# An expert MLP kernel on one Trainium2 core: the second expert chunk by seven products, the sums of x built in two parts

## The chip, the cores and the metric

The kernel runs on one core of a Trainium2 chip. The metric is device time in microseconds (us) of one execution. The kernel before took 957.64 us, the median of three runs (957.54 to 958.07).

## The reference

Three layers follow one another, on 1536 tokens of 512 numbers. The first is attention in which a query sees the keys of its own cluster; the second is a mixture of 4 experts, weighted by normalised probabilities; the third is a plain two-layer network with a leaky ReLU.

```python
def _moe_ref(x, domain_probs, w1, w2):
    N, D = x.shape                  # 1536, 512
    E = w1.shape[0]                 # 4 experts, F = 1024 hidden units each
    p = domain_probs / (domain_probs.sum(-1, keepdims=True) + 1e-09)
    out = np.zeros((N, D), dtype=np.float32)
    for e in range(E):
        h = np.maximum(x @ w1[e], 0.0)
        out += p[:, e:e + 1] * (h @ w2[e])
    return out.astype(np.float32)

def _moe2_ref(x, w_in, w_out):      # 2048 hidden units
    h = x @ w_in
    g = np.maximum(0.01 * h, h)
    return (g @ w_out).astype(np.float32)

def reference(**kwargs):
...
    x = np.ascontiguousarray(attn_out.transpose(0, 2, 1, 3)).reshape(B * S, H * D)
    x = _moe_ref(x=x, **moe_kwargs)
    return _moe2_ref(x=x, **moe2_kwargs)
```

## The kernel before, in words

Numbers are float32; every large product is done as three matmuls on halves of 16 bits (high x high, high x low, low x high). After the heads of the attention, which take the first 255 us or so, the hidden units of both networks are worked off in 24 chunks of 256: chunks 0 to 15 are the experts' (N1 = 16), 16 to 23 the last network's. Each chunk has a hidden part and an outputs part.

**Hidden part.** A chunk in PLAIN goes through `plain` (L1070): for each of three blocks of 512 tokens (`tokens` cuts them) and two halves of 128 hidden units 12 matmuls of 512 columns, so 72. Chunk 0 is such a chunk; its first two blocks are worked off among the last heads, and its third one behind them. The other chunks go through `emit_seven`: hidden units, input rows and tokens (two halves of HT = 768) are each cut in two, and seven products of half-size matrices take the place of eight. `product` (L1059) issues 6 matmuls for one product. The first factors of four products are sums of weights s1 to s4, the second ones of the four are sums of x, t1 to t4, and the remaining products take quarters of the weights and of x as they are. Slices A (512 tokens of each half) and B (256 of each half) are two matmul groups of one product. Where a chunk isn't `full`, only A goes by products, and `plain_b` does the other 512 tokens by 12 matmuls for each half of the hidden units.

**Hidden values.** `h_act` (VectorE, L790) applies the ReLU and the probabilities pb; ScalarE (L139) makes the high half hhi, POOL (L140) the low half hlo.

**Outputs part.** `emit_y1` (L1195 to L1197) makes 12 tiles of 6 matmuls; ScalarE (L1203, chunk 0) or VectorE (L1205, the others) takes each into acc.

**Weights.** SP loads w1 and w2 of a chunk (L190) into w1raw and w2raw. `peak` (ScalarE, L220, into junk) finds the largest value in each partition, a matmul (L224) spreads it, VectorE (L228 to L212) makes a power of two of it, ScalarE scales by it (L272) and makes the high half (L264), POOL the low half (L267). For `emit_seven` POOL builds the four sums of weights (`weights_sums`, L284 to L287), and `split_halves` makes their halves shi (ScalarE, L264) and slo (POOL, L267). The raw buffer of w1 is free for the next load after L287.

**Sums of x.** `input_sums` (L1003) builds f, g and e, by VectorE (L1013) in float32, and their high halves by ScalarE (L1016), low halves by VectorE (L1013). f and g lie in raw64, two tiles of the pool `ffn` that take up memory of the heads' pool after it is closed (L954); the high and low half of e overwrite the quarter b12 of x, xx in the trace.

**Order of work.** The steps of weights and sums are lists of small functions. The loop over the chunks pops some after each block or output tile, by numbers in `quota`; each engine then runs its instructions in the order in which they were issued. Chunk 0 spreads the 18 steps of the sums by `quota = [0, 9, 6, 3]`: none in chunk 0's hidden part, nine among its outputs, six in chunk 1's hidden part and three among its outputs.

In the trace `junk`, `g`, `hhi` and so on are tiles, `z` a bank of PSUM, `big` a wider part of it.

Of the kernel before, what the change touches and what calls it, by code (L numbers as in the profile page):

```python
# [8 lines left out]
F32 = mybir.dt.float32  # L9
# [4 lines left out]
AF = mybir.ActivationFunctionType  # L14
# [61 lines left out]
def attention_moe_kernel(  # L76
# [13 lines left out]
    nc = tc.nc  # L90
# [92 lines left out]
    def weights_load(c, part):  # L183
        wa, wb, f0, e = chunks[c]
        r, n = (raw64, 2) if wide and e is None else (raw12, 1)
        if part == 0:
            src = wa[:, n * f0:n * (f0 + FCH)]
        else:
            src = wb[f0:f0 + FCH, :]
        nc.sync.dma_start(out=r[part], in_=src.rearrange("(k p) f -> p k f", p=128))  # L190
# [597 lines left out]
    def h_act(c, g, src, p):  # L788
        if c < N1:
            nc.vector.scalar_tensor_tensor(out=g, in0=src, scalar=0.0, in1=p, op0=ALU.max, op1=ALU.mult)  # L790
        else:
            nc.scalar.activation(out=g, in_=src, func=AF.Prelu, scale=H_DOWN, alpha=0.01)
# [9 lines left out]
    def like(x, y):  # L802
        return x if len(y.shape) == 2 else x.rearrange("p (u t) -> p u t", u=2)
# [196 lines left out]

    t_hi, t_lo = [[t[:, 0], t[:, 1], quarters[1][n], t[:, 2]] for n, t in enumerate((thi, tlo))]

    def input_sums():  # L1003

        sub, add = ALU.subtract, ALU.add
        b11, b12, b21, b22 = quarters
        f, g = [
            x.bitcast(F32).rearrange("p a b -> p (a b)")[:, 0:NT].rearrange("p (k t) -> p k t", k=2) for x in raw64
        ]
        e = part  # L1010

        def tt(out, in0, in1, op):
            return lambda: nc.vector.tensor_tensor(out=out, in0=in0, in1=in1, op=op)  # L1013

        def hi(n, src):
            return lambda: nc.scalar.activation(out=t_hi[n], in_=src, func=AF.Copy)  # L1016

        def lo(n, src):
            return tt(t_lo[n], src, t_hi[n], sub)

        return [
            tt(f, b12[0], b11[0], sub), tt(f, f, b12[1], add), tt(f, f, b11[1], sub),
            hi(0, f), tt(g, b22[0], f, sub), tt(g, g, b22[1], add), lo(0, f), hi(1, g), tt(e, b22[0], b12[0], sub),
            tt(e, e, b22[1], add),
            lo(1, g), tt(e, e, b12[1], sub), tt(f, b21[0], g, sub), tt(f, f, b21[1], add), hi(3, f),
            hi(2, e), lo(3, f), lo(2, e),
        ]

    def turn_sums(m):
# [44 lines left out]
    def emit_seven(c, steps, late):  # L1074
# [12 lines left out]
        u2, u3 = [{A: part[:, n, A], B: part[:, n, B]} for n in range(2)]  # L1087
        gB = [g_slot(2), g_slot(3)]

        full = c < N1 or c >= FULL  # L1090
        calls = [5 if full else 6]

        def some():
# [19 lines left out]
        def plain_b(f):  # L1113

            ps = bank(f)
            xs = [x.rearrange("p k (u t) -> p k u t", u=2) for x in (xhi, xlo)]
            for k in range(KC):
                for i, j in ((0, 0), (0, 1), (1, 0)):
                    nc.tensor.matmul(
                        ps.rearrange("p (u t) -> p u t", u=2), lhsT=w[i][:, k, 128 * f:128 * f + 128],  # L1120
                        rhs=xs[j][:, k, :, 512:HT], start=k + i + j == 0, stop=k == KC - 1 and i == 1,
                    )
            h_act(c, gB[f], ps, None)
            hi, lo = [x[:, f, :].rearrange("p (u t) -> p u t", u=2)[:, :, 512:HT] for x in hbuf[0]]
            split(hi, lo, gB[f].rearrange("p (u t) -> p u t", u=2), nc.gpsimd)

# [151 lines left out]
    def mixed(*lists):  # L1278
        return [x for row in zip_longest(*lists) for x in row if x]

    PLAIN = (0, 1, N1, N1 + 1)
    FULL = N1 + 4
    sums_left, quota = [], []
    for c in range(NCH):
# [14 lines left out]
        if c in PLAIN:  # L1299
            if c != N1:  # L1300
                if c > 0:
                    weights_split(c, 1)
                out_scale(c)
            if c == N1:
                sums_left = turn_sums(slice(0, 512))
                quota = [0, 6, 4, 3]
            if c == 0:
                sums_left = input_sums()
                quota = [0, 9, 6, 3]
            n = quota.pop(0)  # L1310
            slots = mixed(sums_left[:n], steps)
            slots[len(slots) // 2:len(slots) // 2] = late[:1]
            if c != N1:
                slots += late[1:]
            sums_left = sums_left[n:]
            if c == N1:
                turn_max(1)
                for k in range(KC):
                    turn_split(1, k)
                weights_split(c, 1)  # L1320
            blocks = [(u, f) for u in range(2 if c == 0 else 0, NU) for f in range(NF)]
            for n, (u, f) in enumerate(blocks):
                if c > 0 and c != N1:
                    ps = bank(BANKS[u][f])
                    plain(c, u, f, ps)
                elif f == 0:
                    both_ps = [bank((BANKS[u] if c else LAST_BANKS)[f]) for f in range(NF)]
                    for k in range(KC):
                        for g in range(NF):
                            plain(c, u, g, both_ps[g], [k])  # L1330
                if c == N1 and n == 0:
                    turn_across(1, bank(1))
                    turn_scale(1)
                    for k in range(KC):
                        turn_split(2, k)
                    out_scale(c)
                if c == 0 or c == N1:
                    ps = both_ps[f]
                h_whole(c, f, ps, 512 * u, hl=[tokens(x[:, f], c, u, True) for x in hbuf[0]])
                if c == N1 and n < 2:  # L1340
                    continue
                for _ in range(-(-len(slots) // (len(blocks) - n))):
                    slots.pop(0)()
            left = []
        else:
            emit_seven(c, steps, late)
            left = steps

        steps, later = left, []
        if c == N1 + 2:  # L1350
            sums_left = turn_sums(slice(512, HT))
            quota = [5, 8]
        if c in PLAIN or N1 + 2 <= c < FULL:
            n = quota.pop(0)
            later, sums_left = sums_left[:n], sums_left[n:]
        if more:
            if not is_wide(c + 1):
                later.insert(0, lambda: peak(c + 1, 1))
            else:
                if c + 1 != N1:  # L1360
                    later.insert(0, lambda: peak(c + 1, 1))
                if c == N1:
                    later = late[1:] + later
                if c + 2 < NCH:
                    later.append(lambda: weights_load(c + 2, 1))
            if L1_POINT(c):
                steps.append(lambda: weights_split(c + 1, 0))
            else:
                steps.insert(0, None)
            if c + 1 not in PLAIN:  # L1370
                steps += weights_sums()
            if c + 2 < NCH and not is_wide(c + 2):
                steps.append(lambda: weights_load(c + 2, 0))
        if c == N1 - 3 and wide:
            steps += [lambda: weights_load(N1, 0), lambda: weights_load(N1, 1)]
        if c < N1 - 1 and c % (FE // FCH) == FE // FCH - 1:
# [66 lines left out]
```

## Time and profile before

| | |
|---|---|
| median of three runs | 957.64 us |
| profiled execution, device time | 957.7 us |
| its span, first to last instruction | 955.8 us |
| TensorE busy | 98% of the span |
| share of the chain that ended last | TensorE 84%, VectorE 11% |
| granted TensorE clock | full speed in every slice |
| chunk 0's third block | 250.02 to 255.20 us |
| chunk 0's outputs | 255.20 to 270.85 us |
| chunk 1's hidden part, its outputs | 270.85 to 286.39, 286.39 to 302.04 us |

The span is taken by the hardware profiler; the device time of the same execution has 1.9 us around it. Busy times are sums of an engine's instructions; the rows further down show when each engine worked, and "idle before" with an arrow names what ended the idle time. A duration is that of one instruction or, with x2 or more behind it, of several in a row, and neighbouring instructions of one engine can overlap by up to 0.1 us.

### The profile page before, as it was taken

What the parts mean: (1) busy time and instruction counts of PE and PEld (TensorE: products, weight loads), DVE (VectorE), ACT (ScalarE), POOL (GpSimd) and SP (SyncE); (2) the same over time, 40 slices, a digit from 0 to 9 for tenths busy, and PEclk for the clock granted to TensorE, in tenths of its full rate; (3) what the DMA queues carried; (4) which work ended last, traced back from release to release, by engine and by line L of the source; (5) the groups of instructions that cost most, each with busy time, mean ns of one, the idle gap of its engine ahead of it and who ended that gap; (6) DMA issues with size and microseconds to landing.
All of it is one profiled execution on the core that took longest, in us unless ns stands there. A gap on an engine that the chain in (4) does not pass through costs nothing.

```text
span 955.8 us, 16375 instructions
## 1 busy us (share of the span) xinstructions
PE 938.0 (98%) x6423; PEld 552.2 (58%) x6456; DVE 749.0 (78%) x1286; ACT 536.8 (56%) x775; POOL 564.1 (59%) x456
## 2 busy tenths in 40 slices
PE   8899999999999999999999999999999999999998
PEld 5788888877545555555555555555544444455554
DVE  7989998889697676666766667666889978998865
ACT  3678777778555344334344343443579755566552
POOL 4467777780367565455654465654636667777672
PEclk9999999999999999999999999999999999999999
DMA  8785556550110112110211102114111211221103
GB/s 181 182 186 120 129 131 156 122 135 3 45 45 25 42 47 54 45 45 23 61 40 45 45 23 75 37 33 132 45 45 59 94 54 60 88 89 45 45 1 132
DMA packets 62245, 70.81 MB, mean 74 GB/s; under 512 B 28148, under 2 KB 44920, under 8 KB 62168
## 3 DMA queue, kind: packets, MB, share of 16 engines
q1 hardware_dynamic: 62168, 69.77, 27.0%
q8 instruction: 50, 0.82, 0.4%
q14 instruction: 27, 0.22, 0.1%
HBM read 46.19 MB, written 3.17 MB: 52 GB/s over the span
## 4 chain that ended last, share of the span: by engine, by line
PE 84%; DVE 11%; ACT 2%; DMA 1%; issue 1%; SPq 0%; DVEq 0%; ACTq 0%
PE z L1059 27%; PE z L1195 9%; PE z L1196 8%; PE z L1197 8%; PE z L1257 4%; PE z L1259 4%; PE z L1258 4%; PE z L1070 4%; PE big L508 3%; DVE m L512 2%; PE big L543 2%; PE big L544 2%; PE small L569 1%; PE small L570 1%; PE small L571 1%
## 5 line engine op out<-in xcount | busy, mean ns | idle before, releaser
L140 POOL TENSOR_TENSOR hlo<-g,hhi 128x512 bf16<-128x512 f32 x140 | 186.4, 1354 | 89.9 <-ACT hhi L139 89.9
L1205 DVE SCALAR_TENSOR_TENSOR acc<-z,outer,acc 128x512 f32<-128x512 f32 x180 | 133.8, 748 | 64.7 <-PE z L1197 64.7
L557 POOL TENSOR_TENSOR plo<-p,phi 128x768 f16<-128x768 f32 x83 | 136.2, 1652 | 68.3 <-ACT phi L556 38.6
L139 ACT ACTIVATE hhi<-g 128x512 f16<-128x512 f32 x140 | 86.6, 628 | 111.8 <-DVE g L790 110.2
L1195 PE MATMUL z<-hhi,w2hi 128*128 128x512 f16 x384 | 145.5, 379 | 1.6
L1196 PE MATMUL z<-hhi,w2lo 128*128 128x512 f16 x384 | 145.5, 379 | 0.0
L267 POOL TENSOR_TENSOR w2lo<-w2raw,w2hi 128x512 f16<-128x512 f32 x46 | 63.5, 1400 | 131.5 <-ACT w2hi L264 131.5
L1197 PE MATMUL z<-hlo,w2hi 128*128 128x512 bf16 x353 | 133.8, 379 | 0.0
L512 DVE TENSOR_REDUCE m<-big 128x1 f32<-128x768 f32 x96 | 89.9, 950 | 14.0 <-PE big L508 13.7
L546 ACT ACTIVATE p<-big 128x768 f32<-128x768 f32 x96 | 76.6, 808 | 34.6 <-PE big L544 28.6
L1059 PEld LDWEIGHTS <-shi 128*128 128x128 f16 x608 | 59.5, 98 | 41.3 <-issue 0.2
L1099 DVE TENSOR_TENSOR part<-z,part 128x512 f32<-128x512 f32 x76 | 41.2, 563 | 50.9 <-PE z L1059 48.3
L267 POOL TENSOR_TENSOR w1lo<-w1raw,w1hi 128x512 f16<-128x512 f32 x46 | 57.4, 1270 | 28.5 <-ACT w1hi L264 18.8
L1059 PE MATMUL z<-xx,shi 128*128 128x512 f16 (+1 forms) x304 | 73.1, 329 | 0.1
L1257 PE MATMUL z<-w2hi,hhi 128*128 128x512 f16 (+1 forms) x194 | 73.1, 377 | 0.1
L1059 PE MATMUL z<-xx,w1hi 128*128 128x512 f16 (+1 forms) x304 | 73.1, 329 | 0.0
L1259 PE MATMUL z<-w2hi,hlo 128*128 128x512 f16 (+1 forms) x194 | 73.1, 377 | 0.0
L1258 PE MATMUL z<-w2lo,hhi 128*128 128x512 f16 (+1 forms) x194 | 73.1, 377 | 0.0
L543 PE MATMUL big<-qka 128*128 128x512 f32 x192 | 70.0, 367 | 2.8 <-DVE m L512 1.2
L1266 DVE SCALAR_TENSOR_TENSOR accn<-z,outer,accn 128x512 f32<-128x512 f32 (+1 forms) x85 | 60.2, 736 | 14.5 <-PE z L1259 14.4
L264 ACT ACTIVATE shi<-sums 128x1024 f16<-128x1024 f32 x20 | 21.1, 1057 | 88.4 <-POOL sums L287 88.4
L790 DVE SCALAR_TENSOR_TENSOR g<-z,pb 128x512 f32<-128x512 f32 x92 | 51.7, 568 | 19.2 <-PE z L1059 11.4
(250 smaller groups left out, 2342.7 us busy)
## 6 DMA issues: line engine op xcount, KB each, us to landing
qkb<-pair SPq DMA_DIRECT2D x32, 384.0 KB
w1raw<-in_moe_w_dram SPq DMA_DIRECT2D x16, 512.0 KB
w2raw<-in_moe_w_dram SPq DMA_DIRECT2D x16, 512.0 KB
w1raw<-in_moe_w_in_dram SPq DMA_DIRECT2D x8, 1024.0 KB
w2raw<-in_moe_w_out_dram SPq DMA_DIRECT2D x8, 1024.0 KB
qka<-pair SPq DMA_DIRECT2D x16, 384.0 KB
qraw<-in_q_dram SPq DMA_DIRECT2D x16, 192.0 KB
kraw<-in_k_dram SPq DMA_DIRECT2D x16, 192.0 KB
```

The source lines that it names most:

```text
L140: lo_engine.tensor_tensor(out=lo, in0=src, in1=as_read(hi), op=ALU.subtract)
L267: nc.gpsimd.tensor_tensor(out=lo[:, x], in0=src[:, x], in1=hi[:, x], op=ALU.subtract)
L512: nc.vector.tensor_reduce(out=m_t[t][:, j:j + 1], in_=ps[:, 0:S], op=ALU.max, axis=AX.X)
L557: (nc.vector if plo_on_vector else nc.gpsimd).tensor_tensor(out=plo, in0=p, in1=phi, op=ALU.subtract)
L1059: nc.tensor.matmul(ps, lhsT=w[i][:, k, :], rhs=x[j][:, k, sub], start=first and k + i + j == 0, stop=k == 1 and i == 1, skip_group_check=True,
L1195: nc.tensor.matmul(out, lhsT=whi[:, f, ks], rhs=h, start=f == 0, stop=False)
L1196: nc.tensor.matmul(out, lhsT=wlo[:, f, ks], rhs=h, start=False, stop=False)
L1197: nc.tensor.matmul(out, lhsT=whi[:, f, ks], rhs=l, start=False, stop=f == NF - 1)
L1205: nc.vector.scalar_tensor_tensor(out=a, in0=out, scalar=by, in1=a, op0=ALU.mult, op1=ALU.add)
L1257: nc.tensor.matmul(ps, lhsT=hi[:, f, ts], rhs=whi[:, f, m], start=f == 0, stop=False)
L1258: nc.tensor.matmul(ps, lhsT=hi[:, f, ts], rhs=wlo[:, f, m], start=False, stop=False)
L1259: nc.tensor.matmul(ps, lhsT=lo[:, f, ts], rhs=whi[:, f, m], start=False, stop=f == NF - 1)
```

## The change

Chunk 1 leaves PLAIN and goes through `emit_seven`, but not `full`: slice A by seven products, the other 512 tokens by `plain_b`, whose `h_act` is now given the probabilities in expert chunks. The sums of x are built by `input_sums(m)` for a slice m of the tokens. Slice A is built in chunk 0: its first five steps ahead of the third block, the other 13 among the outputs (quota 16). Slice B is built in chunk 1: eight steps in the hidden part, ten among the outputs. e lies in acc_n instead of part. The sums of weights of chunk 1 are built among chunk 0's outputs, so the load of chunk 2's w1 goes out after them.

```diff
@@ -1000,30 +1000,29 @@
 
     t_hi, t_lo = [[t[:, 0], t[:, 1], quarters[1][n], t[:, 2]] for n, t in enumerate((thi, tlo))]
 
-    def input_sums():
+    def input_sums(m):
 
         sub, add = ALU.subtract, ALU.add
-        b11, b12, b21, b22 = quarters
-        f, g = [
-            x.bitcast(F32).rearrange("p a b -> p (a b)")[:, 0:NT].rearrange("p (k t) -> p k t", k=2) for x in raw64
+        b11, b12, b21, b22 = [[x[:, :, m] for x in b] for b in quarters]
+        f, g, e = [
+            x.rearrange("p a b -> p (a b)")[:, 0:NT].rearrange("p (k t) -> p k t", k=2)[:, :, m]
+            for x in [*[r.bitcast(F32) for r in raw64], acc_n]
         ]
-        e = part
 
         def tt(out, in0, in1, op):
             return lambda: nc.vector.tensor_tensor(out=out, in0=in0, in1=in1, op=op)
 
         def hi(n, src):
-            return lambda: nc.scalar.activation(out=t_hi[n], in_=src, func=AF.Copy)
+            return lambda: nc.scalar.activation(out=t_hi[n][:, :, m], in_=src, func=AF.Copy)
 
         def lo(n, src):
-            return tt(t_lo[n], src, t_hi[n], sub)
+            return tt(t_lo[n][:, :, m], src, t_hi[n][:, :, m], sub)
 
         return [
             tt(f, b12[0], b11[0], sub), tt(f, f, b12[1], add), tt(f, f, b11[1], sub),
-            hi(0, f), tt(g, b22[0], f, sub), tt(g, g, b22[1], add), lo(0, f), hi(1, g), tt(e, b22[0], b12[0], sub),
-            tt(e, e, b22[1], add),
-            lo(1, g), tt(e, e, b12[1], sub), tt(f, b21[0], g, sub), tt(f, f, b21[1], add), hi(3, f),
-            hi(2, e), lo(3, f), lo(2, e),
+            tt(g, b22[0], f, sub), hi(0, f), tt(g, g, b22[1], add), tt(e, b22[0], b12[0], sub), hi(1, g),
+            tt(e, e, b22[1], add), lo(1, g), tt(e, e, b12[1], sub), lo(0, f), hi(2, e),
+            tt(f, b21[0], g, sub), tt(f, f, b21[1], add), lo(2, e), hi(3, f), lo(3, f),
         ]
 
     def turn_sums(m):
@@ -1087,7 +1086,7 @@
         u2, u3 = [{A: part[:, n, A], B: part[:, n, B]} for n in range(2)]
         gB = [g_slot(2), g_slot(3)]
 
-        full = c < N1 or c >= FULL
+        full = 1 < c < N1 or c >= FULL
         calls = [5 if full else 6]
 
         def some():
@@ -1120,7 +1119,11 @@
                         ps.rearrange("p (u t) -> p u t", u=2), lhsT=w[i][:, k, 128 * f:128 * f + 128],
                         rhs=xs[j][:, k, :, 512:HT], start=k + i + j == 0, stop=k == KC - 1 and i == 1,
                     )
-            h_act(c, gB[f], ps, None)
+            if c < N1:
+                p = pbuf[0][:, 0, :].rearrange("p (u t) -> p u t", u=2)[:, :, 512:HT]
+                h_act(c, like(gB[f], p), like(ps, p), p)
+            else:
+                h_act(c, gB[f], ps, None)
             hi, lo = [x[:, f, :].rearrange("p (u t) -> p u t", u=2)[:, :, 512:HT] for x in hbuf[0]]
             split(hi, lo, gB[f].rearrange("p (u t) -> p u t", u=2), nc.gpsimd)
 
@@ -1278,7 +1281,7 @@
     def mixed(*lists):
         return [x for row in zip_longest(*lists) for x in row if x]
 
-    PLAIN = (0, 1, N1, N1 + 1)
+    PLAIN = (0, N1, N1 + 1)
     FULL = N1 + 4
     sums_left, quota = [], []
     for c in range(NCH):
@@ -1305,8 +1308,10 @@
                 sums_left = turn_sums(slice(0, 512))
                 quota = [0, 6, 4, 3]
             if c == 0:
-                sums_left = input_sums()
-                quota = [0, 9, 6, 3]
+                sums_left = input_sums(slice(0, 512))
+                for _ in range(5):
+                    sums_left.pop(0)()
+                quota = [0, 16]
             n = quota.pop(0)
             slots = mixed(sums_left[:n], steps)
             slots[len(slots) // 2:len(slots) // 2] = late[:1]
@@ -1343,6 +1348,11 @@
                     slots.pop(0)()
             left = []
         else:
+            if c == 1:
+                sums_left = input_sums(slice(512, HT))
+                steps = steps[1:] + sums_left[:2] + steps[:1] + sums_left[2:8]
+                quota = [10]
+                sums_left = sums_left[8:]
             emit_seven(c, steps, late)
             left = steps
 
@@ -1350,7 +1360,7 @@
         if c == N1 + 2:
             sums_left = turn_sums(slice(512, HT))
             quota = [5, 8]
-        if c in PLAIN or N1 + 2 <= c < FULL:
+        if c < 2 or c in PLAIN or N1 + 2 <= c < FULL:
             n = quota.pop(0)
             later, sums_left = sums_left[:n], sums_left[n:]
         if more:
@@ -1371,6 +1381,8 @@
                 steps += weights_sums()
             if c + 2 < NCH and not is_wide(c + 2):
                 steps.append(lambda: weights_load(c + 2, 0))
+            if c == 0:
+                steps = [None] * 4 + steps[1:5] + steps[6:] + [None] * 4 + steps[5:6]
         if c == N1 - 3 and wide:
             steps += [lambda: weights_load(N1, 0), lambda: weights_load(N1, 1)]
         if c < N1 - 1 and c % (FE // FCH) == FE // FCH - 1:
```

Three places show how instructions move. The first is VectorE from the end of the heads (L822) to chunk 0's first steps among the outputs; p, g and outer are tiles of hidden values and scales. Before:

```order
L236 TENSOR_SCALAR outer_3529<-pk_3527,pk_3528,most 128x1
L790 SCALAR_TENSOR_TENSOR g_3522<-z_4349,pb_3523 128x512
L790 SCALAR_TENSOR_TENSOR g_4323<-z_4350,pb_3523 128x512
L228 TENSOR_REDUCE pk_3527<-z_4400 128x1
L205 TENSOR_SCALAR pk_3527<-pk_3527 128x1
L209 TENSOR_SCALAR pk_3527<-pk_3527 128x1
L212 RECIPROCAL pk_3527<-pk_3527 128x1
L1013 TENSOR_TENSOR w1raw_4329<-xx 128x1536
L1013 TENSOR_TENSOR w1raw_4329<-w1raw_4329,xx 128x1536 x2
```

After, with the semaphores that each waits for (a repeated row is one instruction more):

```order
L822 SCALAR_TENSOR_TENSOR p<-big_4265,pb_3523 128x512 [waits Pool_49]
L236 TENSOR_SCALAR outer_3529<-pk_3527,pk_3528,most 128x1
L1013 TENSOR_TENSOR w1raw_4329<-xx 128x2x512 [waits DMAHW1_49,DMAHW7_49,DMAHW0_49,Pool_49]
L1013 TENSOR_TENSOR w1raw_4329<-w1raw_4329,xx 128x2x512 [waits DVE_49] x2
L1013 TENSOR_TENSOR w2raw_4330<-xx,w1raw_4329 128x2x512 [waits DVE_49]
L790 SCALAR_TENSOR_TENSOR g_3522<-z_4354,pb_3523 128x512 [waits PE_49]
L790 SCALAR_TENSOR_TENSOR g_4323<-z_4355,pb_3523 128x512 [waits PE_49]
```

Four steps (three of f in w1raw, one of g in w2raw) of 128x2x512 now stand ahead of the two readings of the third block, and the first of them also waits for a count of POOL's.

The second place is ScalarE in chunk 0's outputs and at the start of chunk 1, after the change (L1206 is the former L1203, L1132 evacuates chunk 1's first product):

```order
L1016 ACTIVATE thi<-w1raw_4329 128x2x512
L139 ACTIVATE hhi_3520<-g_3522 128x512
L220 ACTIVATE junk,pb_3525<-w1raw 128x1024
L139 ACTIVATE hhi_3520<-g_4323 128x512
L1206 ACTIVATE acc<-z_4388,outer_3529 128x512
L220 ACTIVATE junk,pb_3526<-w2raw 128x1024
L1206 ACTIVATE acc<-z_4397,outer_3529 128x512
L272 ACTIVATE w1raw<-w1raw,pk_3527 128x1024
L264 ACTIVATE w1hi_3514<-w1raw 128x1024
L1206 ACTIVATE acc<-z_4417,outer_3529 128x512
L1016 ACTIVATE thi<-w2raw_4330 128x2x512
```

The first high half (L1016) stands ahead of the split of g and of the peak L220; before, L139 was followed by L220 with no L1016 ahead. Further on:

```order
L1016 ACTIVATE thi<-w1raw_4329 128x2x512
L1206 ACTIVATE acc<-z_4510,outer_3529 128x512
L264 ACTIVATE shi<-sums 128x1024
L1132 ACTIVATE part<-z_4522 128x512
L272 ACTIVATE w2raw<-w2raw,pk_3528 128x1024
```

The split of the sums (shi) stands behind the high half of t4 and an output. The third place is POOL in the same stretch. Before:

```order
L140 TENSOR_TENSOR hlo_3521<-p,hhi_3520 128x512 x4
L140 TENSOR_TENSOR hlo_3521<-g_3522,hhi_3520 128x512
L140 TENSOR_TENSOR hlo_3521<-g_4323,hhi_3520 128x512
L267 TENSOR_TENSOR w1lo_3515<-w1raw,w1hi_3514 128x512 x2
L267 TENSOR_TENSOR w2lo_3517<-w2raw,w2hi_3516 128x512 x2
L140 TENSOR_TENSOR hlo_3521<-g_4323,hhi_3520 128x512
```

After:

```order
L140 TENSOR_TENSOR hlo_3521<-p,hhi_3520 128x512 x4
L140 TENSOR_TENSOR hlo_3521<-g_3522,hhi_3520 128x512
L140 TENSOR_TENSOR hlo_3521<-g_4323,hhi_3520 128x512
L267 TENSOR_TENSOR w1lo_3515<-w1raw,w1hi_3514 128x512 x2
L284 TENSOR_TENSOR sums<-w1raw 128x256
L285 TENSOR_TENSOR sums<-sums,w1raw 128x256
L286 TENSOR_TENSOR sums<-w1raw 128x256
L287 TENSOR_TENSOR sums<-w1raw,sums 128x256
L267 TENSOR_TENSOR slo<-sums,shi 128x512 x2
L267 TENSOR_TENSOR w2lo_3517<-w2raw,w2hi_3516 128x512 x2
```

The four sums of weights and the halves of them now stand between the two splits of chunk 1's weights. On TensorE chunk 1 has 66 hidden matmuls in the place of 72.

## Rows read from the trace of the kernel before

**Rows 1.** The page: busy time, the granted clock in 40 slices, the chain by engine.

```profile
PE 938.0 (98%) x6423; PEld 552.2 (58%) x6456; DVE 749.0 (78%) x1286; ACT 536.8 (56%) x775; POOL 564.1 (59%) x456
...
PEclk9999999999999999999999999999999999999999
...
PE 84%; DVE 11%; ACT 2%; DMA 1%; issue 1%; SPq 0%; DVEq 0%; ACTq 0%
```

**Rows 2.** Windows: start:end length, each engine's busy time (instructions), granted clock, DMA share, GB/s.

```profile
core 0: us, PE busy (x) PEld busy (x) DVE busy (x) ACT busy (x) POOL busy (x), PEclk, DMA share, GB/s
250.02:255.20 5.18, 5.18 (x25) 2.35 (x24) 1.92 (x4) 1.23 (x2) 3.96 (x4) 1.00 0.00 0
255.20:270.85 15.65, 15.54 (x73) 7.16 (x74) 13.50 (x12) 13.99 (x21) 6.26 (x4) 1.00 0.11 35
270.85:286.39 15.54, 15.54 (x73) 7.05 (x72) 14.54 (x17) 7.52 (x12) 12.10 (x5) 1.00 0.09 34
286.39:302.04 15.65, 15.54 (x73) 7.16 (x74) 13.21 (x23) 7.39 (x8) 12.48 (x10) 1.00 0.01 2
```

**Rows 3.** The chain of waits, 225 to 310 us: start, length, engine, tile, line, count.

```profile
271.02 15.54 PE z L1070 x72
```

**Rows 4.** TensorE's timeline: start, length, line, operation, shapes, count [idle before, releaser].

```profile
1.39 3.40 PE L633 MATMUL small<-zeros 128*128 128x512 bf16 x9 [1.39 <-POOL zeros L619]
...
35.93 0.50 PE L543 MATMUL big<-qka 128*128 128x512 f32 x1 [0.80 <-DVE pair L140]
...
257.79 0.22 PE L224 MATMUL z<-identb,pb 128*128 128x128 bf16 x1
257.85 0.38 PE L1195 MATMUL z<-hhi,w2hi 128*128 128x512 f16 x1
```

**Rows 5.** VectorE's timeline, chunk 0's third block.

```profile
254.75 1.40 DVE L790 SCALAR_TENSOR_TENSOR g<-z,pb 128x512 f32<-128x512 f32 x2 [3.06 <-PE z L1070]
258.05 0.29 DVE L228 TENSOR_REDUCE pk<-z 128x1 f32<-128x128 f32 x1 [1.90 <-PE z L224]
```

**Rows 6.** ScalarE's timeline, chunk 0's third block and outputs.

```profile
255.48 0.63 ACT L139 ACTIVATE hhi<-g 128x512 f16<-128x512 f32 x1 [3.30 <-DVE g L790]
256.02 1.04 ACT L220 ACTIVATE junk<-w1raw 128x1024 bf16<-128x1024 f32 x1
256.96 0.19 ACT L220 ACTIVATION_READ_ACCUMULATOR junk<-w1raw 128x1 f32 x1
...
259.75 1.14 ACT L272 ACTIVATE w1raw<-w1raw,pk 128x1024 f32<-128x1024 f32 x1
260.93 1.06 ACT L264 ACTIVATE w1hi<-w1raw 128x1024 f16<-128x1024 f32 x1
261.89 1.83 ACT L1203 ACTIVATE acc<-z,outer 128x512 f32<-128x512 f32 x3
```

**Rows 7.** POOL's timeline, from the heads' end to chunk 2.

```profile
249.48 4.50 POOL L140 TENSOR_TENSOR hlo<-p,hhi 128x512 bf16<-128x512 f32 x4 [31.29 <-ACT hhi L139]
...
262.06 3.95 POOL L267 TENSOR_TENSOR w1lo<-w1raw,w1hi 128x512 f16<-128x512 f32 x2 [3.15 <-ACT w1hi L264]
...
296.94 0.72 POOL L284 TENSOR_TENSOR sums<-w1raw 128x256 f32<-128x256 f32 x1
297.74 2.13 POOL L285 TENSOR_TENSOR sums<-sums,w1raw 128x256 f32<-128x256 f32 x1
...
302.41 2.27 POOL L267 TENSOR_TENSOR slo<-sums,shi 128x512 f16<-128x512 f32 x2 [1.17 <-ACT shi L264]
```

**Rows 8.** VectorE's timeline, steps of the sums of x, and chunk 2's readings.

```profile
258.83 1.74 DVE L1013 TENSOR_TENSOR w1raw<-xx 128x1536 f32<-128x1536 f16 x1
...
265.03 2.60 DVE L1013 TENSOR_TENSOR w2raw<-xx,w1raw 128x1536 f32<-128x1536 f16 x1
267.66 1.76 DVE L1013 TENSOR_TENSOR w2raw<-w2raw,xx 128x1536 f32<-128x1536 f32 x1
...
305.56 1.08 DVE L1099 TENSOR_TENSOR part<-z,part 128x512 f32<-128x512 f32 x2 [2.05 <-PE z L1059]
```

**Rows 9.** SP's queue, and windows over the load of chunk 2's w1.

```profile
266.04 0.37 SPq L190 DMA_DIRECT2D w1raw<-in_moe_w_dram  x1
...
266.04:270.10 4.06, 4.01 (x20) 1.92 (x20) 4.03 (x3) 4.01 (x7) 0.00 (x0) 1.00 0.40 129
```

## The prediction

> **What bounds the kernel now.** I read the page first, then the stretch from the end of the heads to chunk 2 stage by stage, then the chain of waits there, then each engine's timeline. The page shows TensorE busy for 98% of the span, holding 84% of the chain that ended last, at a granted clock of full speed in all 40 slices [rows 1]. The four stages that the change touches are chunk 0's third token block, its outputs, chunk 1's hidden products and its outputs; in each the matmuls fill all of the time (15.54 of 15.54 or 15.65) while VectorE has 1 to 2.5 us to spare, and more in the first [rows 2]. The chain through chunk 1's hidden products is its 72 matmuls and nothing else [rows 3]. So a removed matmul is worth its full length, and every wait put on TensorE is lost in full: nothing downstream gives it back, since the chunks behind are also matmul after matmul.
>
> **What is removed.** Chunk 1's 72 hidden matmuls take 15.54, 0.216 each [rows 3]. After the change there are 7 products of 6 (42) and two blocks of 12 for the other 512 tokens (24), all 512 columns wide: 66. That is 6 x 0.216 = **-1.29**.
>
> **What is moved ahead of chunk 0's third block.** Before, VectorE went from the heads' last piece straight to the two readings of that block (L790, 1.40 for two), the first at 254.75 [rows 5]; ScalarE's split of the first (L139) began at 255.48, the peak of the weights (L220) ran from 256.02 to 257.15 [rows 6], and TensorE's L224, which needs that peak, came in its turn at 257.79 [rows 4], 0.64 later. Now three steps of f and one of g stand ahead of L790, and L139 and L220 behind hi(0) and the first L790. The peak sits on TensorE's in-order queue, so its slack of 0.64 is all the cover there is.
>
> The first step's target lies where the last p tiles of the heads were, and it waits for POOL's last split of them: four in a row from 249.48, over at 253.98 [rows 7]. It starts at about 254.05. No step of 1024 elements is in the trace. A reading of 512 is 0.70 [rows 5]; a step of 1536 is 1.74 to 1.76 alone [rows 8]. Between these ends I take the straight line, 1.22 (0.70 and 1.74 are the bounds). Four of them with 0.03 between dependent ones end at 259.04. L790 of the first tile then ends at 259.65, L139 (0.63) at 260.30, L220 (1.04 and its accumulator's read) at 261.35, and L224 follows at 261.49. **Wait: 261.49 - 257.79 = +3.70.** With steps of 0.70 it would be 1.6, with 1.74 it would be 5.8; POOL is idle there, so no other work enters.
>
> **What chunk 1 needs before its third product.** Before, chunk 1 read only x and its own weights. Now product s2 x t2 needs the sums of weights split by ScalarE (shi), and by POOL (slo), and those sums were made in nobody's way only from chunk 2 on. Chunk 1 now starts at 270.85 + 3.70 = 274.55; its first product (6) and its plain block (12) cover 18 x 0.216, so shi is wanted at 278.43.
>
> From 261.3 ScalarE runs, in the new order, L139, an output, the peak of w2, an output, L272 (1.14), L264 (1.06) [rows 6], an output and hi(1), which is as long as L264: with 0.6 per output (three took 1.83 [rows 6]) some 6.5 in all, since neighbouring rows overlap by up to 0.1, so hi(1) ends at about 267.8. From there VectorE runs lo(1), an e step, lo(0) and the first f step of t4, while POOL makes the four weight sums. These hinder each other: a VectorE step with two sources in SBUF took 2.60 beside POOL's w1lo, where 1.76 is usual [rows 8]; a weight sum took 2.13 beside such a step and 0.72 alone [rows 7]; w1lo took 3.95 for two beside steps, slo 2.27 alone [rows 7]. In each the excess is about the rest of the other's instruction. The Trainium skill, page SBUF — State Buffer, section Who interferes with whom, has the rule: a VectorE instruction with two SBUF inputs and a GpSimd one that reads SBUF hold the shared ports one at a time, for a whole instruction. By that rule, the rows agree (2.60 against 1.76); by independent ports the three later waits would go, which is the second rival.
>
> Beside a sum of 0.72 a step of 1.22 becomes about 1.75 (the step beside w1lo gained 0.84 of a half's 1.14, so I take three quarters of 0.72). Four of them: 267.78 + 7.0 = 274.8. The four small VectorE instructions of a peak (258.05 to 258.83 before) take 0.8 [rows 5, 8], the last f step 1.22, hi(3) on ScalarE 1.05, an output 0.55, and then shi 1.06, in that order on their queues: 279.3, and 0.1 to TensorE. **Wait +1.0** (0 if the steps stayed at 1.22; 2 if each lost a whole sum). slo's first half is POOL's 1.14 [rows 7] and some 0.35 behind a VectorE step of B: 280.9, and 0.1 to TensorE, which has two matmuls with shi to do first and wants it at 279.9: **wait +1.1** (0.8 alone, 2 behind whole steps).
>
> **Inside chunk 1** VectorE also has ten steps of B, readings of 0.54 to 0.7 (L1099 took 1.08 for two [rows 8]) and POOL beside it. I expect the reading of the bank that the last product re-uses to come 0.7 late and the first output 0.1: **+0.9**, the softest term, with bounds 0 and 3.
>
> **At nothing:** the 13 other A steps, under chunk 0's outputs, except as above; e in accn instead of part; B's remaining steps, which chunk 2 wants more than 15 us later, under chunk 1's outputs, where VectorE has 2.4 of 15.65 free [rows 2] and half-size steps replace whole ones. If that cover went, chunk 2 would wait by the deficit, inside the upper end. SP's load of chunk 2's w1 goes out when POOL's last sum has read the buffer, about 275.5 instead of 266.04 [rows 9]; its 512 KB came in 4.06 at 129 GB/s [rows 9], so it is there by 279.6, and the peak that reads it stands in ScalarE's queue at about 282.4.
>
> **Sum.** 3.7 + 1.0 + 1.1 + 0.9 - 1.3 = **+5.4**. The profiled execution was 957.7 with a span of 955.8; that gives 963.1 and a span of 961.2. The median, 957.64, is 0.06 below that execution, so the forecast is **963.0**.
>
> **A rule that speaks against the change further.** The longest idle time of TensorE's that the rows show is 0.80 [rows 4], and its granted clock is never under full speed [rows 1]; the new wait is four times as long. The nine matmuls at the very start, after 1.39 of nothing, took 3.40, 0.38 each instead of 0.216 [rows 4]: a slow start cost 9 x 0.16 = 1.5. The Trainium skill, page TensorE: Matmul & The Clock Gate, section HAM oscillation, says that a wait between bursts of matmuls can send the clock back to its lower level, and the work behind starts slow. By that rule the result would be 963.0 + 1.5 = 964.5; no row of this trace has such a wait, so it is a rival and not the forecast.
>
> **The rivals.**
> - *The first step is not held, and the steps are short.* If f starts when VectorE is free, at 251.70, and a step takes 0.9 or less, the four are done by 255.35, L790 is 0.6 late, L224 keeps its turn, and all else is 3.7 earlier than above, so that the sums are there by 278.43. Then only the matmuls count: 957.64 - 1.29 = **956.35**. Against it: 0.9 is below the line between 0.70 and 1.74, and the buffer's last reader is POOL [rows 7]. It decides at 255.35. Chance 0.05.
> - *The first step is not held, at 1.22, with independent ports.* The steps end at 256.65 and L790 is 1.9 later than before; 0.64 of that is slack, so the wait is 1.3, the products give 1.3 back: **957.7**, no change. Chance 0.06.
> - *VectorE and POOL do not hinder each other with 1024 elements.* Only the first wait stays: 957.64 + 3.7 - 1.3 = **960.0**. Against it stand the rows above. Chance 0.13.
> - *The clock falls in the first wait*: **964.5**. Chance 0.10.
> - *The later waits pile up*: each of the three later terms at its upper bound (2, 2 and 3) adds 4 in all; half of that gives **965**. Chance 0.10.
> - *The change does not do what it says*: the order of instructions has 66 matmuls for 72, so I give that nothing.
>
> The forecast as worked out has the other 0.56, with 961.2 to 964.5 as its own range (first wait 3.0 to 4.2, the later ones together 1.9 to 4.4).
>
> **How the numbers follow.** What a measurement here can tell from no change is about 0.2%, 1.9. Within it (955.7 to 959.6) lie the first two rivals, the first with a gain of 1.3 that is too small to count as faster, most of their 0.11: 0.10. Faster by more than that needs the first rival and a gain in chunk 1's outputs that no row shows: 0.03. Slower is the rest, 0.87. The range reaches from 959.8, which takes in the case of independent ports, to 965.6, half an us past the piled-up waits and one past the fallen clock; what is outside is the first two rivals and some 0.05 above.
>
> **What would show it.** In the profile of the changed kernel: L224 at about 261.5 with a TensorE gap of some 3.7 before it, released by ScalarE's L220; four VectorE steps of about 1.22 from 254.05 ahead of L790; 66 hidden matmuls in chunk 1; gaps of about 1 before the first matmuls with shi and slo, at 279.4 and 281.0; VectorE steps of 1.6 to 2.0 where POOL makes sums; chunk 2 beginning at about 307.4 (302.05 before); and the granted clock still at full speed. A first step that starts at 251.7, or an L224 within 1 us of its turn, would make the prediction wrong, and so would matmuls of 0.43 behind the wait.

## The result and the profile after

The changed kernel took 963.35 us, the median of six runs (962.79 to 963.94), against 957.54 (957.11 to 958.07) for the kernel before in the same comparison: ratio 1.0058, 95% interval 1.0048 to 1.0069. It is slower by 5.8 us. The span of the profiled execution is 961.3 us instead of 955.8.

The page after, busy times and the chain by engine, beside [rows 1]:

```profile
PE 941.9 (98%) x6450; PEld 552.4 (57%) x6450; DVE 756.3 (79%) x1305; ACT 538.7 (56%) x781; POOL 564.5 (59%) x462
...
PE 83%; DVE 11%; ACT 3%; DMA 1%; issue 1%; POOL 0%; SPq 0%; DVEq 0%; ACTq 0%
```

The page tells little: TensorE is 98% busy as before, and busier in us although it has six matmuls fewer (6450 weight loads, PEld, for 6456; the 6423 matmuls on the page of before are too few, since some records of matmuls are missing there). TensorE's timeline in chunks 0 to 2 tells more (columns as in [rows 4]):

```profile
257.59 0.38 PE L1200 MATMUL z<-hlo,w2hi 128*128 128x512 bf16 x1
261.38 0.29 PE L224 MATMUL z<-identb,pb 128*128 128x128 bf16 x1 [3.41 <-ACT junk L220]
261.46 0.63 PE L1198 MATMUL z<-hhi,w2hi 128*128 128x512 f16 x1
261.88 0.63 PE L1199 MATMUL z<-hhi,w2lo 128*128 128x512 f16 x1
...
277.32 0.60 PE L1058 MATMUL z<-xx,w1hi 128*128 128x512 f16 x2
...
281.21 0.38 PE L1058 MATMUL z<-thi,shi 128*128 128x512 f16 x1
...
290.12 0.38 PE L1118 MATMUL z<-xx,w1lo 128*128 128x512 f16 x1
290.68 0.59 PE L1058 MATMUL z<-xx,shi 128*128 128x512 f16 x2 [0.18 <-DVE g L1098]
...
292.83 0.38 PE L1199 MATMUL z<-hhi,w2lo 128*128 128x512 f16 x1
293.17 0.38 PE L1200 MATMUL z<-hlo,w2hi 128*128 128x512 bf16 x1
...
307.69 0.59 PE L1058 MATMUL z<-xx,w1hi 128*128 128x512 f16 x2
```

A matmul starts 0.216 us after the one before, so L224 was due at 257.81 and came 3.57 late. (Waits are counted here in this way, from start to start; the brackets count from the end of the matmul before and show less.) But the matmul behind it takes 0.63 instead of 0.38, and the next one starts 0.42 later instead of 0.216. The windows over the next stretch, columns as in [rows 2], show why:

```profile
258.00:262.00 4.00, 0.62 (x3) 0.35 (x4) 2.51 (x4) 3.25 (x6) 1.18 (x2) 0.80 0.00 0
262.00:266.00 4.00, 4.00 (x11) 1.40 (x10) 3.87 (x6) 3.97 (x6) 1.13 (x1) 0.50 0.00 0
266.00:270.00 4.00, 4.00 (x17) 1.70 (x16) 2.89 (x3) 3.24 (x6) 3.77 (x3) 0.85 0.00 0
270.00:275.00 5.00, 5.00 (x26) 2.29 (x25) 4.96 (x4) 3.35 (x6) 4.92 (x4) 1.00 0.02 3
```

After the wait the granted clock is 0.50, the lower of its two levels (1.2 of 2.4 GHz). TensorE is "busy" all the time but starts 9 or 10 matmuls in 4 us where 18 or 19 are usual. Chunk 1 began at 277.32, 6.47 later than the 270.85 of [rows 2]: 3.57 for the wait, so 2.90 for the clock. From there to chunk 2 it was 0.83 faster than before (307.69 - 277.32 = 30.37 against 302.05 - 270.85 = 31.20): the six matmuls give 1.29 back, a wait for a bank takes 0.35 (290.68), one for a low half 0.12 (293.17). Sum: 3.57 + 2.90 + 0.35 + 0.12 - 1.29 = 5.65, against 5.64 in the start of chunk 2 and 5.5 in the span.

VectorE's timeline, from the heads' end and in the middle of chunk 0's outputs, answers to [rows 5, 8]:

```profile
254.02 1.23 DVE L1013 TENSOR_TENSOR w1raw<-xx 128x1024 f32<-128x1024 f16 x1 [2.31 <-POOL hlo L140]
255.28 2.48 DVE L1013 TENSOR_TENSOR w1raw<-w1raw,xx 128x1024 f32<-128x1024 f32 x2
257.80 1.23 DVE L1013 TENSOR_TENSOR w2raw<-xx,w1raw 128x1024 f32<-128x1024 f16 x1
258.94 1.28 DVE L790 SCALAR_TENSOR_TENSOR g<-z,pb 128x512 f32<-128x512 f32 x2
...
269.74 1.74 DVE L1013 TENSOR_TENSOR accn<-accn,xx 128x1024 f32<-128x1024 f32 x1
271.40 1.75 DVE L1013 TENSOR_TENSOR tlo<-w1raw,thi 128x1024 f16<-128x1024 f32 x1
273.19 1.63 DVE L1013 TENSOR_TENSOR w1raw<-xx,w2raw 128x1024 f32<-128x1024 f16 x1
```

The first step waits for POOL, a step of 1024 takes 1.23 alone and 1.63 to 1.75 where POOL makes the weight sums. ScalarE's split of the sums, however, waits for nobody and nobody waits for it:

```profile
278.33 1.06 ACT L264 ACTIVATE shi<-sums 128x1024 f16<-128x1024 f32 x1
```

It ends at 279.39; TensorE came to the product that reads it only at 281.21, as the timeline above shows. The two waits of 1.0 and 1.1 that were forecast for shi and slo are not in this profile. So there are two theories. **A:** they were only hidden, since the slow clock made chunk 1 start 2.9 us late. **B:** the wait for L224 and the clock are the whole loss, and the rest of the schedule has room.

### The profile page after: what moved, and what is told of

It reads as the page before. It is cut to its first block, busy times and chain, and to the rows that moved or that the text cites. A ratio compares the mean times of both kernels' runs of the same rounds, so it can differ in the third digit from the quotient of the medians.

```text
span 961.3 us, 16427 instructions
## 1 busy us (share of the span) xinstructions
PE 941.9 (98%) x6450; PEld 552.4 (57%) x6450; DVE 756.3 (79%) x1305; ACT 538.7 (56%) x781; POOL 564.5 (59%) x462
## 4 chain that ended last, share of the span: by engine, by line
PE 83%; DVE 11%; ACT 3%; DMA 1%; issue 1%; POOL 0%; SPq 0%; DVEq 0%; ACTq 0%
PE z L1058 28%; PE z L1198 9%; PE z L1200 9%; PE z L1199 9%; PE z L1260 4%; PE z L1262 4%; PE z L1261 4%; PE big L508 3%; DVE m L512 2%; PE big L543 2%; PE big L544 2%; PE z L1069 2%; PE z L1118 1%; PE small L569 1%; PE small L570 1%; PE small L571 1%
## 5 line engine op out<-in xcount | busy, mean ns | idle before, releaser
L140 POOL TENSOR_TENSOR hlo<-g,hhi 128x512 bf16<-128x512 f32 x140 | 182.4, 1323 | 97.9 <-ACT hhi L139 94.5
L1200 PE MATMUL z<-hlo,w2hi 128*128 128x512 bf16 x384 | 146.6, 382 | 0.0
L139 ACT ACTIVATE hhi<-g 128x512 f16<-128x512 f32 x140 | 86.5, 628 | 106.7 <-DVE g L790 105.1
L267 POOL TENSOR_TENSOR w2lo<-w2raw,w2hi 128x512 f16<-128x512 f32 x46 | 61.3, 1352 | 126.7 <-ACT w2hi L264 126.7
L1058 PE MATMUL z<-xx,shi 128*128 128x512 f16 (+1 forms) x312 | 75.5, 330 | 0.2 <-DVE g L1098 0.2
L1058 PE MATMUL z<-xx,w1hi 128*128 128x512 f16 (+1 forms) x312 | 75.5, 330 | 0.0
L267 POOL TENSOR_TENSOR w1lo<-w1raw,w1hi 128x512 f16<-128x512 f32 x46 | 55.0, 1217 | 26.1 <-ACT w1hi L264 18.8
L1058 PEld LDWEIGHTS <-w1hi 128*128 128x128 f16 x468 | 45.2, 98 | 35.7
```

The source lines that it names most:

```text
L140: lo_engine.tensor_tensor(out=lo, in0=src, in1=as_read(hi), op=ALU.subtract)
L267: nc.gpsimd.tensor_tensor(out=lo[:, x], in0=src[:, x], in1=hi[:, x], op=ALU.subtract)
L1058: nc.tensor.matmul(ps, lhsT=w[i][:, k, :], rhs=x[j][:, k, sub], start=first and k + i + j == 0, stop=k == 1 and i == 1, skip_group_check=True,
L1200: nc.tensor.matmul(out, lhsT=whi[:, f, ks], rhs=l, start=False, stop=f == NF - 1)
```

## The experiments

**e1_fill.** 16 matmuls into L224's bank, overwritten by it, so that TensorE doesn't stand still.

```diff
+                for _ in range(16 if c == 0 else 0):
+                    nc.tensor.matmul(ps, lhsT=xhi[:, 0, 0:128], rhs=xhi[:, 0, 0:512], start=True, stop=True)
                 peak_across(0, ps)
```

> The changed kernel, with 16 matmuls more on TensorE right ahead of L224 in chunk 0 (3.45 us at full pace, into the bank that L224 then overwrites), so that TensorE does not stand still while it waits for the peak. Theory A (the waits for shi and slo are still there and were only hidden by the slow clock, which made chunk 1 start 2.9 us later): the clock stays at full speed, L224 stays at 261.4, chunk 1 starts near 274.4 and then waits about 1.0 for shi, 1.1 for slo and 0.7 for the bank of the last product; 963.0 us in all, as the changed kernel. Theory B (the slow clock is a loss of its own on top of the first wait, and nothing waits behind it): the clock's 2.9 us come back, 960.5 us.

Measured: 963.79 (963.25 to 964.12), ratio 1.0061 (1.0044 to 1.0077). TensorE's timeline of the profiled execution (963.25):

```profile
257.87 3.62 PE L1404 MATMUL z<-xx 128*128 128x512 f16 x16
261.45 0.23 PE L224 MATMUL z<-identb,pb 128*128 128x128 bf16 x1
...
278.25 0.38 PE L1118 MATMUL z<-xx,w1lo 128*128 128x512 f16 x1
279.48 0.39 PE L1058 MATMUL z<-thi,shi 128*128 128x512 f16 x1 [0.85 <-ACT shi L264]
279.70 0.38 PE L1058 MATMUL z<-tlo,shi 128*128 128x512 f16 x1
281.01 0.39 PE L1058 MATMUL z<-thi,slo 128*128 128x512 f16 x1 [0.93 <-POOL slo L267]
...
289.50 0.38 PE L1118 MATMUL z<-xx,w1lo 128*128 128x512 f16 x1
290.54 0.59 PE L1058 MATMUL z<-xx,shi 128*128 128x512 f16 x2 [0.67 <-DVE g L1098]
```

L224 comes when it did, the clock stays at full speed in this execution, and the hidden waits stand there: from start to start 1.01, 1.09 and 0.83, and 0.13 for a low half. Theory A, its waits met to about a tenth. The clock's 2.9 us are not saved; nearly all of them were spent in a place where TensorE would have waited anyway. The other three executions are 0.5 to 0.9 longer, at a mean clock of 0.998; they have no trace, so where their clock fell is not known.

**e2_late.** The five steps are issued behind the two tiles of the third block, not ahead of them.

```diff
-                for _ in range(5):
-                    sums_left.pop(0)()
-                quota = [0, 16]
+                quota = [5, 18]
```

> The changed kernel with the first five steps of the sums of x issued behind the third block's two tiles instead of ahead of them. Theory A (VectorE, POOL and ScalarE have too much to do before chunk 1's products, so a wait that is moved comes back elsewhere): L224 comes in its turn, but output tiles wait some 2.4 and 0.8 us for ScalarE's queue, chunk 1 waits 1.6 for shi and 1.1 for slo, 0.7 for a bank; 963.0 us, with the granted clock at full speed since no wait is as long as 3.4 us. Theory B (putting the five steps ahead of the block is what costs): the first wait and the slow clock go, and the result is 957.5 - 1.3 + at most 1 = 956.2 to 957.2 us.

Measured: 963.84 (963.03 to 963.95), ratio 1.0058 (1.0043 to 1.0073). TensorE's waits by what ended them (us in total, times, longest), 255 to 295 us:

```profile
PE z L1198 <- ACT acc L1206: 2.8, 2, 2.2
PE z L1058 <- ACT shi L264: 1.3, 1, 1.3
PE z L1058 <- POOL slo L267: 0.9, 1, 0.9
```

The wait for L224 is gone and others are there, from start to start: 2.35 and 0.81 for output tiles, 1.46 for shi, 1.10 for slo. Theory A. Wrong was "full speed", and with it the reason given: the changed kernel's clock fell behind an idle time of 3.41, but here it fell for some 3 us behind the last two waits, which are shorter.

```profile
281.00:285.00 4.00, 3.93 (x11) 1.48 (x12) 2.50 (x3) 2.62 (x5) 4.00 (x5) 0.57 0.01 2
```

By the starts of the matmuls that cost 1.6, and again it took the place of a wait, though a shorter one: the one of 0.7 for the bank is not in this profile. Sum: 5.72 of waits, 1.6 for the clock and 1.29 given back are 6.03, and the median is 6.02 over the kernel before (957.82).

**e3_plain and e4_plain_fill.** Chunk 1 by 72 plain matmuls, the sums of x built as in the change; e4 with the 16 matmuls of e1. Both leave out the weight sums, which a plain chunk doesn't need. In both, chunk 1 reads t3's halves where a quarter of x was, since the sums are made before it; they are kernels for timing alone.

```diff
-    PLAIN = (0, N1, N1 + 1)
+    PLAIN = (0, 1, N1, N1 + 1)
...
+            if c == 1:
+                sums_left = input_sums(slice(512, HT))
+                quota = [8, 10]
...
-            if c == 0:
-                steps = [None] * 4 + steps[1:5] + steps[6:] + [None] * 4 + steps[5:6]
```

> The changed kernel with chunk 1 by its 72 plain matmuls again; the sums of x stay in two parts and their five steps ahead of the third block. Nothing in chunk 1 needs shi or slo now. Theory A: the first wait of 3.6 us and the slow clock (13 matmuls at twice the time, 2.9 us) are seen in full: 957.5 + 3.6 + 2.9 = 964.0 us, and no wait in chunk 1. Rival (the products, not the early steps, are what costs): 957.5 us, within 1 us.

> The kernel of e3_plain with the 16 matmuls of e1_fill ahead of L224. Theory A (the slow clock comes from TensorE's standing still, and costs 2.9 us where nothing hides it): the granted clock stays at full speed, the time falls from 964.0 by 2.9 to 961.1 us, or to 962 if ScalarE's queue then holds up output tiles by 0.8 us. Rival (the slow clock has another cause, or costs nothing): as e3_plain, 964 us.

Measured: e3 963.09 (961.55 to 964.18), ratio 1.0051 (1.0036 to 1.0066); e4 961.47 (961.41 to 962.08), ratio 1.0037 (1.0024 to 1.0050). One window of each, e3 first:

```profile
261.40:267.40 6.00, 5.37 (x18) 2.12 (x19) 4.82 (x7) 5.21 (x9) 1.93 (x2) 0.72 0.28 87
```

```profile
261.40:267.40 6.00, 6.00 (x29) 2.76 (x30) 4.83 (x7) 5.14 (x8) 1.50 (x3) 1.00 0.29 90
```

e4 is as theory A has it. In e3, with nothing behind the first wait that waits in its turn, the slow clock is seen in the time, though it cost less in most executions than the 2.9 expected (some 1.7 in the profiled one, 963.52, by the starts of its matmuls). e3's four executions go by their mean clock: 961.55 at 1.000, 962.67 and 963.52 at 0.998, 964.18 at 0.996. Its median is 1.6 above e4's, the longest 2.7. The changed kernel's six executions do not go by it, as theory A has it: 963.35 at 1.000, 962.79 to 963.94 at 0.998, 963.28 at 0.996. The rival of e3, that the products cost and not the early steps, falls: with plain matmuls and a full clock e4 is still 3.65 over the kernel before (957.82), the first wait alone. The products cost too. Between the profiled executions of e4 and e1, both with the 16 matmuls and at full clock, lie 1.82 (961.43 and 963.25): 3.06 of waits in e1 less the 1.29 that the six matmuls give back is 1.77.

**e5_no_weight_sums.** e1 without POOL's four weight sums; the products that use them work on zeros.

```diff
-                steps = [None] * 4 + steps[1:5] + steps[6:] + [None] * 4 + steps[5:6]
+                steps = [None] * 7 + [lambda: nc.gpsimd.memset(sums, 0.0)] + steps[6:] + [None] * 4 + steps[5:6]
```

> The kernel of e1_fill with POOL's four sums of the weights of chunk 1 left out (one memset of the tile stands in their place, so chunk 1's four products with weight sums work on zeros, and their splits are made as before). Theory A (VectorE's steps and POOL's sums hold each other up, one whole instruction at a time): the four VectorE steps between 268 and 275 us take 1.22 instead of 1.75, the wait for shi of 1.0 goes, the one for slo stays at 1.1 to 1.2 and the bank's at 0.8; 963.2 - 1.0 = 962.3 us by the profiled execution. Rival (the steps are long for another reason, or POOL alone is slowed): the steps stay at 1.75, shi comes at the same time, 963.2 to 963.8 us.

Measured: 961.42 (961.32 to 961.60), ratio 1.0038 (1.0025 to 1.0051), 2.4 under e1. Between the profiled executions, both at full clock, it is 1.65 (961.60 and 963.25). VectorE's timeline for the steps that are 269.74 to 273.19 above:

```profile
269.71 1.21 DVE L1013 TENSOR_TENSOR accn<-accn,xx 128x1024 f32<-128x1024 f32 x1
270.85 1.21 DVE L1013 TENSOR_TENSOR tlo<-w1raw,thi 128x1024 f16<-128x1024 f32 x1
272.10 1.22 DVE L1013 TENSOR_TENSOR w1raw<-xx,w2raw 128x1024 f32<-128x1024 f16 x1
```

1.21 instead of 1.74: shown, VectorE's steps wait for POOL's sums. shi was ready at 277.83 (279.42 in e1), its wait is gone, and slo's is down to 0.69. So 1.4 of the 1.65 are waits, more than the 1.0 expected, because slo came earlier too, where its wait was expected to stay. The rest of the 2.4 is not traced: three of e1's four executions had a mean clock of 0.998, all five of e5 had 1.000, and the two were compared with other executions of the kernel before (957.82 and 957.55). The first of the four steps, beside w1lo, stayed at 2.12, as it should.

**e6_peak_early.** The peak of w1 ahead of the five steps.

```diff
+                steps.pop(0)()
                 for _ in range(5):
```

> The changed kernel with the peak of chunk 1's w1 (L220) issued on ScalarE ahead of the five early steps, so that L224 finds it done. Theory A (a wait that is taken away comes back at the next engine that is late): L224 comes in its turn at 257.8 us, but output tiles then wait 1.8 and 0.5 for ScalarE's queue, which stands behind the high halves of the sums, and chunk 1 waits 1.6 for shi, 1.1 for slo and 0.7 for the bank; 957.5 + 5.8 - 1.3 = 962.1 us, the granted clock at full speed up to chunk 1. Theory B (L220's place behind the early steps is what costs): without the first wait and the slow clock 957.0 us or less.

Measured: 962.60 (961.69 to 963.27), ratio 1.0051 (1.0034 to 1.0068). TensorE's waits, 255 to 295 us:

```profile
PE z L1198 <- ACT acc L1206: 2.0, 2, 1.6
PE z L1058 <- ACT shi L264: 1.3, 1, 1.3
PE z L1058 <- POOL slo L267: 0.9, 1, 0.9
PE z L1058 <- DVE g L1098: 0.7, 1, 0.7
```

No wait for L224, and four others: 1.72 and 0.59, 1.46, 1.09, 0.82 from start to start. Theory B falls here most plainly: its one change was to take the first wait away.

**e7_reordered.** The same steps in the best order that I found by replaying the queues (working each engine's instructions off in order, with measured durations); a0 to a17 are the sums of x in their order, p the peaks, x the spread and w the split that follow, l1 and ld the loads, s and sp the weight sums and their split, the lists by place (ahead of the block, behind its two tiles, behind each output tile). In `product` the two matmuls with the low half of the weights come last, and six steps of B instead of eight stand in chunk 1's hidden part.

```diff
+                for k in ['a0', 'l1', 'a1', 'p0', 'a2']:
+                    c0[k]()
...
+                    for k in [['p1', 'a3'], ['a4']][n]:
...
+                for k in [['a5'], ['x0', 'w0', 'a6', 's1'], ['a11', 'a7'], ['a8', 'a9', 'a13'], ['s2'], [], ['s3', 's4'], [], [], ['a14', 'a10', 'x1'], ['a16', 'a17', 'a12', 'sp'], ['a15', 'ld']][i]:
```

> The changed kernel with the same steps in another order: ahead of the third block three steps of f with the peak of w1 between them, the two peaks and the split of w1 as early as their engines allow, the weight sums from the second output tile on, the high halves behind the output tiles that can go first, six steps of B in chunk 1's hidden part instead of eight; and in every product the two matmuls with the low half of the weights last. Theory A (VectorE and POOL together have too much to do ahead of chunk 1's products, so that the best order leaves part of the waits): no first wait, full clock, one wait of 1.4 of an output tile for ScalarE's queue and one of 1.3 for slo; 957.5 + 2.65 - 1.3 = 958.9 us, 4.4 less than the changed kernel and still not faster than before. Theory B (only the order of the change is at fault): no wait is left, 956.3 us.

Measured: 959.03 (958.58 to 959.25, 11 runs), ratio 1.0013 (1.0004 to 1.0022), the clock at 1.000 in all. The waits that are left, 255 to 303 us:

```profile
PE z L1197 <- ACT acc L1205: 1.4, 1, 1.4
PE z L1057 <- POOL slo L267: 0.7, 1, 0.7
```

Each against the kernel before of its own comparison, 1.33 us are left (959.03 - 957.70) of the 5.81, so order is worth some 4.5; it did not make the products pay. From start to start the two waits are 1.56 and 0.88, where 1.4 and 1.3 were expected. No order that was run beats the kernel before. That none exists is not shown.

## Why the prediction was right, and where it was not

**The time** was forecast at 963.0, with a range of 959.8 to 965.6, and measured at 963.35; the chance of slower was 0.87. The sign and the first wait were right by their mechanism; the size also had luck, as the paragraph on the clock says. The sign stands on what e1, e2 and e6 show: chunk 1's products need steps of VectorE, POOL and ScalarE that in this order are not finished in time, and TensorE, which has no other wait there, loses what they are late.

**The products:** -1.29. In the changed kernel chunk 1 to chunk 2 is 0.83 shorter with 0.47 of waits, so 1.30.

**The first wait:** forecast 3.70, measured 3.57. The first step was to start at 254.05, behind POOL's last split, and did at 254.02; a step of 1024 was taken as 1.22 from a straight line between 0.70 and 1.74 and is 1.23. L224 was forecast at 261.49 and came at 261.38. What fell with this are the rivals with a step that is not held (956.35 and 957.7). The working of the first of them had a slip: it set the sums, moved 3.7 earlier, against a wanted time of 278.43 that was not moved; with both moved the sums (275.6) come 0.9 behind the wanted time (274.7), unless the shorter steps make that up.

**The later waits:** forecast +1.0, +1.1 and +0.9. They are the step that failed for the changed kernel as it ran: its profile has 0, 0 and 0.47. As a statement on the engines they were right: e1 has 1.01, 1.09 and 0.96. What the working left out is that the first wait also slows what comes behind it, and so moves the time at which TensorE wants shi from 278.4 to 281.2.

**The clock** was a rival at 0.10 and happened in the profiled execution: matmuls of 0.43 behind the wait were named as a sign that would make the prediction wrong, and there they were (261.46 to 261.88). Apart from 1.39 at the very start, [rows 4] hold no wait above 0.80, so the trace of before could not decide it. The Trainium skill, page TensorE: Matmul & The Clock Gate, section HAM oscillation, says that a wait between bursts of matmuls can send the clock back. By that rule, the trace agrees: 0.50 behind a wait of 3.57. The rival's time, 964.5, was wrong twice. The price was taken from nine matmuls at the start (1.5) and is 2.9 in the profiled execution, where 13 start some 0.2 late each. And it was added to the later waits, where it takes their place: 3.57 + 2.90 + 0.47 is 6.94, and 3.57 + 3.06 is 6.63 with the clock up. The forecast met the time with the clock missing from it, since the two ways differ by 0.3. That one hides the other is shown by e1; that they come out so nearly equal is luck.

**VectorE and POOL.** The step beside a weight sum was forecast at 1.75 and took 1.63 to 1.75; e5 shows the cause. The rule that the prediction cited from the Trainium skill, page SBUF — State Buffer, section Who interferes with whom, stands with 1.21 without the sums against 1.74 with them. A step grew by 0.53, less than the 0.72 that a sum takes alone, so that each holds the ports for a whole instruction is shown only roughly. The rival without it (960.0) falls; it is the third in the list, where the working calls the case the second.

**Chunk 2** was forecast to begin at 307.4 and began at 307.69; "the granted clock still at full speed" was wrong.

## What to carry to other kernels

Replay each engine's queue in its new order with measured durations, hand-overs included, before you trust a count of saved matmuls: here 1.3 us saved cost some 7 us of waits and slow clock, and a wait taken away at one engine came back at the next. A part that is slowed ahead of a wait may cost nothing, and mending it alone (e1) gives nothing; find the last releaser without it. When a change makes TensorE wait far longer than any wait in the trace, price the slower clock behind it as well, and ask what it hides.

## What the runs showed that I had not expected

The clock's fall differs between executions of one kernel and is not tied to one long wait. Of e3's four executions, which have the same instructions ahead of L224, one had a mean clock of 1.000, two 0.998 and one 0.996, and in the profiled one the first five matmuls behind a wait of 3.57 still went out at full pace and only later ones slowly, 0.43 apart from 263.51 to 266.50; in e2 the clock fell behind waits of 1.46 and 1.10, and in e6's profiled execution waits of 1.46 and 1.09 left it at full speed. What decides was not tried.
